# Four row tiles for two outer products, and three other numbers for the planner that orders the kernel

## The chip, the core and the metric

The kernel runs on one core of one Trainium2 chip. Its time is device microseconds of an execution, and the figure compared is the median of several runs. Of one execution there is also a profile: every instruction of every engine with its start and end. The engines are PE (matrix products), PEld (PE's loading of the stationary operand), DVE and ACT (element by element work), POOL (a slower helper) and SP (issues most transfers).

## The reference

Two branches read the same 2048 tokens of width 640 and are mixed by a gate for each token, `g = sigmoid(sum(x * gate_w))`.

```python
x = A_u
g = _sigmoid((x * gate_w).sum(-1, keepdims=True))
a = _A_ref(x, ...)                     # long convolution
b = relu(x @ w1) @ w2                 # network, 640 -> 1728 -> 640
return g * a + (1 - g) * b

# _A_ref: for each of 640 channels d a filter K[d, l] over l = 0 .. 2047
A = -exp(log_A_real) + 1j * A_imag
C = (C_real + 1j * C_imag) * exp(log_dt)[:, None]
P = exp((A * dt[:, None])[:, :, None] * l)
K = 2 * einsum("dn,dnl->dl", C, P).real        # n = 0 .. 127
y = causal convolution of x with K (by FFT), + x * D_skip
```

Each tap of a filter is a sum over 128 complex exponentials. With l written as 32 a + b (64 values of a, 32 of b) an exponential is a coarse factor in a times a fine factor in b, so a filter is a product of two small matrices of cosines, sines and decays.

## The kernel before

The work falls into three kinds, which share one core and are interleaved by a planner written in the kernel.

**The network** (`feed_forward`; tile names pf, h, hw, w1, w2, q). All its products are split into a high and a low part in a reduced float32 format, three products for one. The 1728 inner features are done in three parts of 5, 5 and 4 blocks of 128. `wide` multiplies x by w1 for 512 tokens (products of 512 columns), ACT takes relu and the high part, DVE the low part; `sums` multiplies by w2 (products of 320 columns) and adds to the running result q, which waits in memory between parts.

**Generating the taps** (`ssm`). The 640 channels go in 40 chunks c of 16. The logarithms and phases of a chunk, split into 8 rows a channel (128 rows), are read back from memory as a tile PS for four chunks at a time (`load_rows`, queue "rows"). `phases` and `exponents` then form, as outer products with a constant table `tg`, for each of the 128 values of n and each channel: pg (64 numbers: 32 fine phases and 32 of 64 coarse ones), px (64: coarse decays) and pe (32: fine decays). The table is block-diagonal: a channel's 8 rows meet its own columns and zeros elsewhere. ACT rounds pg to whole turns (cs, `whole`), DVE subtracts (sn), ACT takes exp of pe and px (me, mg) and sine and cosine, DVE multiplies them into factors (`factors`: G, mg, cs, sn). `taps` multiplies the factors of two chunks (pk), DVE transposes them (kt), POOL adds D_skip, and they go to memory (kd). The products of one chunk, pg, px and pe, stand together ("a visit", 40 of them).

**The convolution** (`conv`). It replaces the FFT by four stages of small products on tiles of the array: `stage1` (operands tf and ck, cl or xu; tiles of 64 rows and 64 columns), `stage2` (tm; 64x32), `inv2` (tn; 32x64) and `inv1` (tw; 128x64), in five blocks of 128 channels. All write tiles called pc. One call of `inv2` issues 64 products, which the profile records as 128, since it shows two for each product in plain float32.

**The order.** The class `Plan` holds tasks with an engine, a queue, an estimated duration, what they wait for, what buffers they take, and a rank. `run` simulates all engines and writes the instructions in the order found; each engine then executes its own in program order, whatever the real times are. PE has a mode for each kind of tiling: "f" for full products, "c" and "c1" for the convolution, "t" for taps; `CHANGE` is what a switch costs in the plan. `run` also counts PE's instructions, in blocks of 128, and lets PE wait in the plan where a block would be used up before the next is fetched (`FETCH`, `BUSY`, lines 274 to 282 before). Transfers land after their size over a `RATE` for their queue. `CG` says for each of eight groups of 256 tokens how many of the five channel blocks are joined on the network's way out (q, POOL in `joined` and `with_last`) and how many on the convolution's (yo, POOL in `inv1`).

PSUM has eight banks: before, pg and px have two each, pe and pk one each, and pf two; the convolution's pc follows where the generation's were.

## Time and profile before

| | |
|---|---|
| median of 3 runs | 622.47 us (621.3 to 626.9) |
| the profiled execution's own time | 632.85 us |
| its span, first to last instruction | 631.1 us |
| granted TensorE clock, mean | 0.992 |
| busy PE, PEld, DVE, ACT, POOL | 609.0, 481.6, 507.9, 399.0, 92.4 us |

The profiled execution is 10.4 us longer than the median. Rows of the profile name an operation by its engine and by the tiles it writes and reads (out<-in). "L322" is one helper line that records every operation, so tiles tell them apart. A bracket behind a row of the timeline is the time for which the engine was idle before, and what ended it; "issue" there means that nothing the profile shows released the engine. A matrix product's end is modelled and products overlap, so the step from one start to the next is what a product costs PE.

### The profile page before, as it was taken

How to read it: one execution, taken by the hardware profiler on the slowest of the kernel's cores; microseconds unless marked ns; L12 is line 12 of the kernel's file. 1: busy time of each engine (PE TensorE's matmuls, PEld its weight loads, DVE VectorE, ACT ScalarE, POOL GpSimd, SP SyncE). 2: the span in 40 equal slices, each digit the busy share in tenths (PEclk: the TensorE clock that was granted, in tenths of full speed). 3: DMA queues.
4: the chain of work that ended last, by engine and by line, in shares of the span. 5: the costliest groups of instructions: out<-in, count | busy, mean ns of one | idle time of the engine just before them, and what ended most of it. 6: DMA issues, size and time to landing. Idle time of an engine off the chain costs nothing.

```text
span 631.1 us, 18316 instructions
## 1 busy us (share of the span) xinstructions
PE 609.0 (97%) x7864; PEld 481.6 (76%) x7864; DVE 507.9 (80%) x794; ACT 399.0 (63%) x579; POOL 92.4 (15%) x133
## 2 busy tenths in 40 slices
PE   7999989999999999999999999999979999989997
PEld 5998969888988988988988988755656465656656
DVE  5998559898999889999999998568676757746842
ACT  6578369997999888788789796023225342342470
POOL 0000000000000000000000000007060180361744
PEclk9999989998999999999999999999999999999999
DMA  9993933913656435535442243781543534563343
GB/s 292 386 371 116 406 102 115 301 58 109 195 184 242 153 108 205 153 112 177 133 144 81 64 162 116 234 339 30 194 127 126 183 103 136 185 221 102 115 149 119
DMA packets 54153, 108.05 MB, mean 171 GB/s; under 512 B 5432, under 2 KB 29880, under 8 KB 53176
## 3 DMA queue, kind: packets, MB, share of 16 engines
q1 hardware_dynamic: 53848, 106.63, 50.4%
q8 instruction: 62, 1.02, 0.7%
q10 hardware_dynamic: 224, 0.25, 0.1%
q14 instruction: 19, 0.16, 0.1%
HBM read 67.79 MB, written 39.06 MB: 169 GB/s over the span
## 4 chain that ended last, share of the span: by engine, by line
PE 78%; DVE 11%; DMA 5%; ACT 3%; issue 2%; POOL 0%; SPq 0%; DVEq 0%; ACTq 0%
PE pf L322 47%; PE pc L322 18%; PE pk L322 6%; PE pg L322 3%; PE px L322 2%; PE pe L322 1%; DMA ws<-in_B_w_dram 1%; DVE hwl L322 1%; DVE mg L322 1%; DVE sn L322 1%; DVE G L322 1%; DMA ps<-hl 1%; DMA xu<-in_x_dram 1%; DMA ws<-in_w_dram 1%; DMA PS<-ps 1%
## 5 line engine op out<-in xcount | busy, mean ns | idle before, releaser
L322 PE MATMUL pf<-xx,w1h 128*128 128x512 f32 x560 | 175.5, 399 | 1.7 <-DVE w1h L322 1.0
L322 PEld LDWEIGHTS pf<-xx,w1h 128*128 128x128 f32 x560 | 102.6, 189 | 37.2 <-issue 12.6
L322 PE MATMUL pf<-xx,w1l 128*128 128x512 f32 x260 | 102.1, 393 | 0.0
L322 ACT COPY ku<-pc 128x512 f32<-128x512 f32 (+1 forms) x60 | 43.8, 758 | 74.0 <-PE pc L322 63.4
L322 POOL TENSOR_TENSOR ku<-ku 128x256 f32<-128x256 f32 x80 | 56.2, 744 | 86.2 <-DVE ku L322 56.8
L322 POOL TENSOR_TENSOR kt<-kt,dsk 128x8 f32<-128x8 f32 x20 | 9.3, 466 | 393.0 <-DVE kt L322 211.6
L322 DVE STREAM_TRANSPOSE ku<-pc 128x512 f32<-128x512 f32 x80 | 50.8, 687 | 15.4 <-PE pc L322 15.2
L322 DVE TENSOR_TENSOR ku<-pc,ku 128x512 f32<-128x512 f32 x80 | 52.8, 686 | 11.0 <-ACT ku L322 9.6
L322 PE MATMUL pf<-w2l,hh 128*128 128x320 f32 x192 | 59.2, 312 | 1.9 <-issue 1.9
L322 PE MATMUL pf<-w2h,hh 128*128 128x320 f32 x192 | 59.7, 315 | 0.8 <-DVE q L322 0.8
L322 PE MATMUL pf<-w2h,hwh 128*128 128x320 f32 x192 | 59.7, 312 | 0.7 <-ACT hwh L322 0.7
L322 PE MATMUL pf<-w2l,hwh 128*128 128x320 f32 x192 | 59.9, 313 | 0.0
L322 PE MATMUL pf<-w2h,hwl 128*128 128x320 f32 x192 | 58.1, 316 | 1.9 <-DVE hwl L322 1.9
L322 ACT CAST cs<-pg 128x1024 int32<-128x1024 f32 x40 | 40.4, 1010 | 29.5 <-PE pg L322 29.4
L322 PEld LDWEIGHTS pf<-xx,w1l 128*128 128x128 f32 x260 | 49.0, 188 | 11.0 <-DVE w1l L322 0.3
L322 DVE TENSOR_TENSOR sn<-pg,cs 128x1024 f32<-128x1024 f32 x40 | 48.6, 1215 | 7.5 <-ACT cs L322 7.4
L322 ACT ACT_TABLE_LOAD x42 | 53.9, 1283 | 0.7
L322 DVE TENSOR_TENSOR mg<-mg,cs 128x1024 f32<-128x1024 f32 x40 | 49.0, 1224 | 2.9 <-ACT cs L322 1.0
L322 PE MATMUL pf<-w2h,hl 128*128 128x320 f32 x160 | 48.1, 317 | 0.0
L322 ACT ACTIVATE cs<-cs,half_pi 128x1024 f32<-128x1024 f32 x40 | 45.7, 1142 | 0.0
L322 PE MATMUL pc<-ku,tm 64*32 64x256 f32 x1280 | 42.9, 392 | 2.7 <-issue 2.4
L322 ACT ACTIVATE mg<-px 128x1024 f32<-128x1024 f32 x40 | 41.3, 1033 | 1.8 <-PE pk L322 1.8
(151 smaller groups left out, 1260.4 us busy)
## 6 DMA issues: line engine op xcount, KB each, us to landing
xx<-xt SPq DMA_DIRECT2D x24, 640.0 KB, 4.7
xt<-xx SPq DMA_DIRECT2D x16, 640.0 KB, 8.8
part<-q SPq DMA_DIRECT2D x16, 640.0 KB, 3.3
q<-part SPq DMA_DIRECT2D x16, 640.0 KB, 4.9
xl<-in_u_r_dram SPq DMA_DIRECT2D x16, 320.0 KB, 3.1
kd<-kt SPq DMA_DIRECT2D x80, 64.0 KB, 2.5
xu<-in_u_b_dram SPq DMA_DIRECT2D x5, 1024.0 KB, 4.9
xu<-in_x_t_dram SPq DMA_DIRECT2D x6, 640.0 KB, 6.8
```

Source lines behind the costliest of these rows:

```text
L322: self._last = self._tc.keep_in_program_order(f(*a, **k))
```

## The change

Four things change together.

1. `phases` issues pg and px as four products, each of 32 rows (4 channels) with 512 columns (64 of pg and 64 of px for each of its 4 channels), into four banks of one tile, where there were two products of 128 rows for pg and two for px. Each of the four uses its own 32 rows of the array. The table holds 4 channels' columns in place of 16, so `tg` falls from 2560 columns to 1024 and `spread`, which builds it on ACT, from 32 instructions to 20. pe stays a full product. ACT's and DVE's readers see the halves of the four banks (`quads`). One tile and one token now stand for pg and px. The visit's first task has a mode "g" of its own.
2. In `run`, where a task of the convolution would be held up by the fetch of instructions for more than `STALL` (0.3), a ready network product is taken in its place; `FETCH` goes from 2.4 to 3.0.
3. Reloads of PS are counted as landing 2.5 us later (`LAND`).
4. `CG` goes from (0,0,0,0,1,2,5,5) to (0,0,0,0,1,3,5,5).

```diff
-CG = (0,0,0,0,1,2,5,5)
+CG = (0, 0, 0, 0, 1, 3, 5, 5)
...
-    FETCH = 2.4
+    FETCH = 3.0
     BUSY = 2.6
     SLACK = .8
-    MARGIN = 0
+    STALL = .3
+    LAND = dict(rows=2.5)
...
+                if e == 'PE' and t.mode in self.BURST and done + t.n >= 128:
+
+                    end = start + t.dur * (128 - done) / t.n
+                    if block + self.FETCH + (self.BUSY if dma > end + 2 else 0) - end > self.STALL:
+                        other = [x for x in c if x[1].mode == 'f' and x[0] <= start + .05]
+                        if other:
+                            r, t = min(other, key=lambda x: key(x[1]))
+                            start = max(at, r)
...
-                t.end = max(dma, start + t.dur) + 1.15 + self.MARGIN
+                t.end = max(dma, start + t.dur) + 1.15 + self.LAND.get(t.q, 0)
...
+        quads = lambda x: x.rearrange("p (m d) j -> p m (d j)", m=4)
...
-                p = self.psg.tile([128, 4, 256], F32, name="pg")
-                pf = p.rearrange("p d j -> p (d j)")
-                st['pg'] = pf.rearrange("p (d j) -> p d j", j=64)
-                for h in range(2):
-                    x = slice(h * 512, h * 512 + 512)
-                    self.E.matmul(pf[:, x], R[c], self.tg[:, x], start=True, stop=True)
+                p = self.psg.tile([128, 4, 512], F32, name="pg")
+                st['pg'], st['px', c] = p[:, :, :256], p[:, :, 256:]
+                for m in range(4):
+                    x = slice(32 * m, 32 * m + 32)
+                    self.E.matmul(p[:, m], R[c][x], self.tg[x, :512], start=True, stop=True)
...
-            a = visit[c, 1] = A('PE', None, 0.46, pe, [rd, opened, *self.tg_done], take=[p_], use=[r_], rank=GPR, mode='f')
+            a = visit[c, 1] = A('PE', None, 0.26, pe, [rd, opened, *self.tg_done], take=[p_, px_], use=[r_], rank=GPR, mode='g', n=4)
...
-                p = self.psg.tile([128, 4, 256], F32, name="px")
-                pf = p.rearrange("p d j -> p (d j)")
-                st['px', c] = pf.rearrange("p (d j) -> p d j", j=64)
-                for h in range(2):
-                    x = slice(h * 512, h * 512 + 512)
-                    self.E.matmul(pf[:, x], R[c], self.tg[:, 1024 + h * 512:1536 + h * 512], start=True, stop=True)
                 q = st['pe', c] = self.psg.tile([128, C, 32], F32, name="pe")
-                self.E.matmul(q.rearrange("p d j -> p (d j)"), R[c], self.tg[:, 2048:], start=True, stop=True)
+                self.E.matmul(q.rearrange("p d j -> p (d j)"), R[c], self.tg[:, 512:], start=True, stop=True)
...
-            a = visit[c, 2] = A('PE', None, 0.69, pe, [rd, opened, *self.tg_done], take=[p_], use=[r_], rank=GPR, mode='f')
+            a = visit[c, 2] = A('PE', None, 0.24, pe, [rd, opened, *self.tg_done], use=[p_, r_], rank=GPR, mode='f', n=1)
```

The planner's order moves on all engines. Three places on PE follow, each before and then after the change. The helper's line is L332 in the changed kernel; pf<-xx are products of `wide`, pf<-w2 products of `sums`, and numbers in names tell buffers apart.

The first place is the first visit of the generation, on PE. Before:

```order
L322 MATMUL pf<-xx,w1h_205 128x512 x2
L322 MATMUL pf<-xx,w1l_206 128x512
L322 MATMUL pg<-tg,PS 128x512 x2
L322 MATMUL px<-tg,PS 128x512 x2
L322 MATMUL pe<-tg,PS 128x512
L322 MATMUL pf<-xx,w1h_205 128x512 x2
L322 MATMUL pf<-xx,w1l_206 128x512
```

After:

```order
L332 MATMUL pf<-xx,w1h_205 128x512 x2
L332 MATMUL pf<-xx,w1l_206 128x512
L332 MATMUL pf<-xx,w1h_205 128x512 x2
L332 MATMUL pf<-xx,w1l_206 128x512
L332 MATMUL pf<-xx,w1h_212 128x512 x2
L332 MATMUL pf<-xx,w1l_213 128x512
L332 MATMUL pg<-tg,PS 128x512 x4
L332 MATMUL pe<-tg,PS 128x512
L332 MATMUL pf<-xx,w1h_212 128x512 x2
L332 MATMUL pf<-xx,w1l_213 128x512
```

The visit has four products of pg in place of two and two, and twelve network products of 512 columns that followed it now stand ahead of it (the rest of the block of w1h_205 and the first three of w1h_212).

The second place is where `inv2` (pc<-ku,tn) of the first channel block meets `stage2` (pc<-ku,tm) of the second, on PE. Before:

```order
L322 MATMUL pc<-ku,tn 64x128 x64
L322 MATMUL pc<-ku,tm 32x256 x48
L322 MATMUL pf<-w2l_4798,w2h_5603 128x320
L322 MATMUL pf<-w2h_4797,w2l_5604 128x320
L322 MATMUL pf<-w2h_4675,hh_5253 128x320
```

After:

```order
L332 MATMUL pc<-ku,tn 64x128 x64
L332 MATMUL pf<-w2l_4783,w2h_5551 128x320
L332 MATMUL pf<-w2h_4782,w2l_5552 128x320
L332 MATMUL pc<-ku,tm 32x256 x48
L332 MATMUL pf<-w2h_4588,hh_5201 128x320
```

Two network products moved from behind the first 48 products of `stage2` to between the two bursts.

The third place is the first half of `inv2` of the fourth channel block, on PE, with the end of `inv1` (pc<-ku,tw) of the block before. Before:

```order
L322 MATMUL pc<-ku,tm 32x256 x32
L322 MATMUL pc<-ku,tw 64x512 x2
L322 MATMUL pf<-w2h_4752,w1l_6728 128x320
L322 MATMUL pf<-w2h_4797,w2h_6753 128x320
L322 MATMUL pf<-w2l_4798,w2h_6753 128x320
L322 MATMUL pf<-w2h_4797,w2l_6754 128x320
L322 MATMUL pc<-ku,tw 64x512 x2
L322 MATMUL pc<-ku,tn 64x128 x64
L322 MATMUL pf<-w2h_4675,hh_6387 128x320
```

After, from the last of the twelve network products that now stand between the halves of the 64:

```order
L332 MATMUL pf<-w2h_4782,w2l_6860 128x320
L332 MATMUL pc<-ku,tn 64x128 x32
L332 MATMUL pf<-w2h_4588,hh_6341 128x320
L332 MATMUL pf<-w2l_4589,hh_6341 128x320
L332 MATMUL pf<-w2h_4588,hl_6342 128x320
L332 MATMUL pf<-w2h_4599,hh_6568 128x320
L332 MATMUL pf<-w2l_4600,hh_6568 128x320
L332 MATMUL pc<-ku,tw 64x512 x8
```

The 64 products of `inv2`, which stood in one burst, are two bursts of 32 with network products between them, and the products of `inv1` follow behind five more.

More of the change, by code (lines that the diff above doesn't have):

```diff
@@ L102, in tables @@
     tg[np.arange(16), :, 160 + np.arange(16)] = 1
+    tg[np.arange(16), :, 176 + np.arange(16) % 4] = 1
     f = lambda x: np.ascontiguousarray(x.astype(np.float32))
-    return dict(t_g=f(tg.reshape(128, 176)), t_f1=f(np.tile(np.stack([f1, f1[slots()]], axis=1), (2, 1, 1))), t_w=f(w.reshape(128, 64)),
+    return dict(t_g=f(tg.reshape(128, 180)), t_f1=f(np.tile(np.stack([f1, f1[slots()]], axis=1), (2, 1, 1))), t_w=f(w.reshape(128, 64)),
                 t_m=f(m.reshape(128, 32, 64)), t_n=f(n.reshape(128, 8, 2, 2, 64)))
@@ L948, in steps_in @@
         def steps_in():
[L949 removed]
+            tl['tgs'] = self.prm.tile([128, 180], F32, name="tgs")
             D_.dma_start(tl['tgs'], io['t_g'])
@@ L962, in params @@
             self.late_loads.append(a)
-        for d in range(0, 16, 2):
-            self.tg_done.append(A('ACT', 'tg', 1.1, spread(range(d, d + 2)), [a], rank=TGA))
+        for d in range(0, 16, 4):
+            self.tg_done.append(A('ACT', 'tg', 1.1 if d else 2.2, spread(range(d, d + 4)), [a], rank=TGA))
         return [*done, *self.tg_done]
```

23 lines of the change are left out of this document (12 added, 11 removed).

## The prediction

> **What bounds the kernel now.** I read the page first, for which engine is full and for how long.
>
> ```profile
> span 631.1 us, 18316 instructions
> PE 609.0 (97%) x7864; PEld 481.6 (76%) x7864; DVE 507.9 (80%) x794; ACT 399.0 (63%) x579; POOL 92.4 (15%) x133
> PE   7999989999999999999999999999979999989997
> DVE  5998559898999889999999998568676757746842
> PE 78%; DVE 11%; DMA 5%; ACT 3%; issue 2%; POOL 0%; SPq 0%; DVEq 0%; ACTq 0%
> ```
>
> PE is busy 97% of the span and carries 78% of the chain that ended last. DVE, with 80% overall, is at 8 or 9 tenths from the sixth slice to the 25th and lower after it. Those are two stages: the taps are generated until about 403 us, then they are convolved. So I split the span there, with the table of busy times by window.
>
> ```profile
> 85.00:160.00 75.00, 73.44 (x844) 63.99 (x843) 67.02 (x95) 67.94 (x86) 1.90 (x4) 0.97 0.40 129
> 160.00:385.00 225.00, 224.26 (x2831) 197.62 (x2829) 215.70 (x323) 196.66 (x224) 6.65 (x14) 1.00 0.45 148
> 385.00:403.40 18.40, 17.88 (x346) 16.66 (x345) 13.55 (x23) 4.02 (x5) 0.57 (x1) 1.00 0.70 212
> 403.40:631.10 227.70, 214.58 (x3439) 134.25 (x3437) 147.41 (x239) 80.66 (x164) 82.41 (x107) 0.99 0.47 155
> 160.00:200.00 40.00, 40.00 (x445) 34.96 (x444) 39.29 (x56) 37.46 (x47) 0.91 (x2) 1.00 0.64 213
> ```
>
> After the window and its length come PE, PEld, DVE, ACT and POOL busy, then the granted clock. In the generation (first three rows, 318.4 us) PE works 73.44 + 224.26 + 17.88 = 315.6 us and DVE 67.02 + 215.70 + 13.55 = 296.3 us. PE is the bound there, but DVE has only 22.1 us of idle time in all. In the convolution (fourth row) DVE has 80 us to spare and PE 13.1 us of visible idle. This is the main fact of the case: work taken from PE in the generation is worth at most what DVE can give back.
>
> **Part 1: phases and coarse decays on four row tiles.** One of the 40 visits, from the timeline of PE:
>
> ```profile
> 212.22 0.62 PE L322 MATMUL pg<-tg,PS 128*128 128x512 f32 x2
> 212.68 0.62 PE L322 MATMUL px<-tg,PS 128*128 128x512 f32 x2
> 213.14 0.40 PE L322 MATMUL pe<-tg,PS 128*128 128x512 f32 x1
> 213.38 0.31 PE L322 MATMUL pf<-w2h,hl 128*128 128x320 f32 x1
> ```
>
> From 212.22 to 213.38 it is 1.16 us: five products of 512 columns at 0.23 us each. Afterwards pg and px come from four products, each on 32 rows of the array, and pe from one full one. No row shows a tile of 32 rows by 128 columns, so the price has to be built. Other tiles show what running side by side and changing the tiling cost:
>
> ```profile
> 409.31 0.39 PE L322 MATMUL pf<-xx,w1l 128*128 128x512 f32 x1
> 409.63 3.71 PE L322 MATMUL pc<-xu,tf 64*64 64x512 f32 x32
> 413.27 0.73 PE L322 MATMUL pf<-xx,w1h 128*128 128x512 f32 x2
> 413.84 0.40 PE L322 MATMUL pf<-xx,w1l 128*128 128x512 f32 x1
> 417.51 0.62 PE L322 MATMUL pf<-xx,w1h 128*128 128x512 f32 x2
> 417.96 0.39 PE L322 MATMUL pf<-xx,w1l 128*128 128x512 f32 x1
> 418.28 1.95 PE L322 MATMUL pc<-ck,tf 64*64 64x512 f32 x16
> 420.16 0.73 PE L322 MATMUL pf<-xx,w1h 128*128 128x512 f32 x2
> ```
>
> Thirty-two records on 64x64 tiles take 3.64 us until the next full product (413.27 less 409.63), sixteen take 1.88 us. Sixteen more, four sets of four tiles, therefore cost 1.76 us: 0.44 us a set. The fixed part inside is 1.88 − 1.76 = 0.12 us. The step into the tiles is 0.32 us instead of 0.23, 0.09 more. After the return two products take 0.57 us (413.27 to 413.84) instead of 0.45 (417.51 to 417.96), 0.12 more. A round trip into tiles and back costs 0.09 + 0.12 + 0.12 = 0.33 us.
>
> The set of four itself: at best one full product's step, 0.23 us; at worst four steps in a row, 0.92 us (the slower rival below). The row nearest in shape says 0.44, but it is in plain float32, while pg, like pf, multiplies in the reduced format of the 0.23 us step. I take 0.23 and keep 0.44 for the range. A visit becomes 0.23 + 0.23 + 0.33 = 0.79 us, which saves 0.37 us, and 40 of them 14.8 us of PE. With 0.44 it would be 0.16 us each, 6.4 us in all. The Trainium skill (TensorE: Matmul & The Clock Gate, Measured speedup vs the span model) gives 3.07 times for four row tiles of 512 columns: 0.92/3.07 = 0.30 us for the set, an estimate from that page, and 2.8 us less in all; no run shows it yet.
>
> ACT and DVE read the same numbers of elements, now from half of each of four banks, and I price that at nothing. The table t_g shrinks twelve ACT copies of it away, in the first 80 us, where ACT is not on the chain; also nothing.
>
> **Part 2: rows counted as landing later.** The first visit waits for its reload:
>
> ```profile
> 80.35 0.39 PE L322 MATMUL pf<-xx,w1l 128*128 128x512 f32 x1
> 82.72 1.11 PE L322 MATMUL pg<-tg,PS 128*128 128x512 f32 x2 [1.98 <-DMA PS<-ps]
> 83.62 1.06 PE L322 MATMUL px<-tg,PS 128*128 128x512 f32 x2
> 84.48 0.63 PE L322 MATMUL pe<-tg,PS 128*128 128x512 f32 x1
> 82.70:86.30 3.60, 3.58 (x9) 2.85 (x10) 1.31 (x2) 2.36 (x3) 0.00 (x0) 0.53 0.05 19
> ```
>
> PE idles 1.98 us and the following nine products run at a granted clock of 0.53, 0.43 us each instead of 0.23: 1.8 us more. The order now puts twelve more products of 512 columns (12 × 0.23 = 2.7 us) ahead of that visit, so both losses should go, 3.8 us of PE. The landing itself does not move, and it is where DVE's share of the generation begins.
>
> **Parts 1 and 2 together.** The 1.98 us lie ahead of the landing. Between it and the last taps PE needs 14.8 + 1.8 + 2.7 = 19.3 us less. DVE's 296.3 us of work stay (the DVE rows of the new order hold the same operations, about 1 us less of them behind the first sn). PE's share would so fit in 318.4 − 19.3 = 299 us, and DVE needs 296.3 with no idle time at all. The two are level, and DVE becomes the bound as often as PE. What it reaches when pressed: 39.29 of 40 us (98.2%) in its best stretch above, 215.70 of 225 (95.9%) over the long one, where PE was the bound. I take 97.2%: 296.3/0.972 = 304.8 us, **13.6 us less** than 318.4; by the two shares 16.7 and 9.4. The 19.3 us of PE are not all paid out: some 6 us turn into waits of PE for sn, G and mg.
>
> **Part 3: network products where instructions are awaited.** PE's waits that nothing releases, in the convolution:
>
> ```profile
> 452.88 0.70 PE L322 MATMUL pc<-ku,tm 64*32 64x256 f32 x16 [1.32 <-issue]
> 471.79 0.99 PE L322 MATMUL pc<-ku,tn 32*64 32x128 f32 x23 [3.22 <-issue]
> 509.32 0.67 PE L322 MATMUL pc<-ku,tm 64*32 64x256 f32 x13 [1.05 <-issue]
> 560.99 0.41 PE L322 MATMUL pf<-w2l,hh 128*128 128x320 f32 x1 [1.94 <-issue]
> 471.90:475.40 3.50, 3.50 (x33) 3.17 (x34) 1.22 (x3) 2.06 (x2) 0.00 (x0) 0.51 0.59 186
> ```
>
> They sum to 7.5 us, and behind the longest the clock is at 0.51 for 3.5 us, another 1.7: 9.2 us at stake. All lie in or just behind bursts of small tiles, as the rule assumes. The order shows two products put before the first wait's place, more around the others, and nothing changed at the longest: inv2 with 14 network products ahead of it and 12 behind, where 15 and 14 stood. I take 4 us for the profiled execution, between 0 and 9.2. Against it stand the new round trips: seven more changes of tiling in the convolution, 7 × 0.33/2 = 1.2 us. The changed CG moves one 128-column piece of two blocks from one POOL join to another; POOL's 82.41 of 227.7 us hide that. If its cover were gone it would be one POOL addition, under 1 us. SP's four more issues stand in queues that wait for data.
>
> **Sum.** The profiled execution has 632.85 us (1.75 around the span): 632.85 − 13.6 − 4 + 1.2 = 616.5. It is 10.4 us over the median of the runs and above the slowest of them, so part of its awaited instructions and clock drops may be its own. For the runs I count only 2.5 us for part 3: 622.47 − 13.6 − 2.5 + 1.2 = 607.6. I forecast **607 us**.
>
> **Rivals.** *A, DVE keeps up:* the stretch of 98.2% speaks for it. Then all 16.7 us come, and with part 3 whole 9.2 − 1.2 on top: 622.5 − 24.7 = 598, or 595 if the tail of the generation closes as well. Against it: the plan reckons DVE's operations shorter than they are (1.14 for sn in the kernel's own text).
>
> ```profile
> L322 DVE TENSOR_TENSOR sn<-pg,cs 128x1024 f32<-128x1024 f32 x40 | 48.6, 1215 | 7.5 <-ACT cs L322 7.4
> L322 ACT CAST cs<-pg 128x1024 int32<-128x1024 f32 x40 | 40.4, 1010 | 29.5 <-PE pg L322 29.4
> ```
>
> *B, the emptying of PSUM decides:* sn takes 1.22 us, cs 1.01, and now pg is free only when sn and mg have both read it. A PE that runs ahead then stops in program order, with network products behind it. At 95.9% for DVE and nothing from part 3: 622.5 − 9.4 + 1.2 = 614; with the set at 0.44 us PE saves only 6.4 + 1.8 + 2.7 = 10.9 us and it is 613 too. The Trainium skill has this as a rule (TensorEngine Tiling (Array Packing), PSUM Bottleneck): tiling speeds up PE and not the emptying of PSUM, which may become the bottleneck. By that rule B is the case, and DVE's 22.1 us of idle time bear it out half.
>
> *C, given back:* network work ahead of the first convolution product is the same in both orders (649 products of 512 columns and 1024 of 320), so the convolution starts earlier by the whole gain, and its loads of kd, q and xx may not; or the rule for instructions does not do what it says, since the longest wait's place is unchanged. Up to the 13.6 us go again: 616 to 623, no change. The DMA share of 0.47 speaks against it.
>
> *D, slower: the four tiles run one after another.* A visit is then 0.92 + 0.23 + 0.33 = 1.48 us, 0.32 more, on a PE that is already the bound: 40 × 0.32 = 12.8 us, and 622.5 + 12.8 − 2.5 = 633. The turning point is a set of 0.60 us (1.16 − 0.23 − 0.33). The 0.44 us for a set of four 64x64 tiles speaks against it; nothing in the profile shows four tiles of 128 columns each.
>
> **Chances.** Forecast (600 to 612) 0.50; A 0.17; B 0.16; C 0.11; D 0.06. A measurement of this kernel tells about 1% (6.2 us) from no change. Faster by more: the first three, less a little of B, 0.82. Within 1%: C and that rest, 0.12. Slower: D, 0.06. The range runs from 595, where A ends, to 618, which takes in B and the lower end of C; outside are the rest of C, D and a better A, about 2 in 10.
>
> **What would show it.** Part 1: pg's four products starting within 0.05 us and a visit near 0.8 us from pg to the next pf; 1.5 us is D. Parts 1 and 2: no wait of PE for PS near 82 us, last kt near 390 us instead of 403, DVE near 97% between, and waits of PE for DVE of several us in all. If DVE is at 95% and PE still never waits, I have the bound wrong. Part 3: waits on issue in the convolution below 4 us in all. The forecast is wrong if the generation shrinks by under 8 us or over 18, or if the convolution's 227.7 us change by more than 6.

## The result, and the profile after

The changed kernel is slower: 646.59 us median of 4 runs (644.88 to 648.06), beside 624.68 us (621.3 to 629.99) for the kernel before on the same chip, a ratio of 1.030 (95% interval 1.026 to 1.035). I had forecast 607 us. Ratios and intervals, here and below, are formed from the single runs in the faster of two states and are not the quotients of the medians beside them (1.035 here).

The profiled execution of the kernel before that the prediction used (632.85 us) was longer than its runs; a second profile of the same kernel, label `again`, took 624.08 us, close to the median, and the stages are compared with that one. The head of the page of the changed kernel:

```profile
span 643.1 us, 18238 instructions
PE 603.3 (94%) x7864; PEld 461.7 (72%) x7864; DVE 508.7 (79%) x794; ACT 397.2 (62%) x567; POOL 92.3 (14%) x133
PE   8999999999979998999999996998999998998897
DVE  5998559898889898999999898677687775955732
```

PE is busy 5.7 us less than the 609.0 of the first profile and the span is 12 us longer: PE waits. The table of busy times by window says in which stage. First the kernel before (the second profile), from the first sn of the generation to the last taps, and from there to the end; then the same two stages of the changed kernel. The columns are those of the prediction's window table.

```profile
84.90:400.00 315.10, 313.16 (x4014) 275.60 (x4014) 296.18 (x439) 268.32 (x314) 9.12 (x19) 1.00 0.46 149
400.00:622.30 222.30, 213.18 (x3438) 133.07 (x3437) 147.26 (x239) 80.67 (x164) 82.50 (x107) 0.99 0.48 158
```

```profile
86.40:414.10 327.70, 305.00 (x4001) 255.32 (x4000) 295.50 (x437) 269.28 (x313) 8.91 (x19) 0.98 0.44 143
414.10:643.10 229.00, 215.85 (x3438) 133.73 (x3436) 147.59 (x239) 81.22 (x164) 82.55 (x107) 0.98 0.47 154
```

Of the 20.8 us between these two executions (644.88 − 624.08), 12.6 come in the generation (327.7 − 315.1), 6.7 in the convolution (229.0 − 222.3) and 1.5 ahead of both (86.4 − 84.9). In the generation PE is busy 8.2 us less, at a granted clock of 0.98 in place of 1.00, and idles 22.7 us in place of 1.9. DVE's work is the same to 0.7 us; its idle time grew from 18.9 to 32.2 us. No engine is full there any more: PE, DVE and ACT wait for each other. The waits of the changed kernel by engine (total, times, longest) name whom for:

```profile
ACT mg L332 <- DVE sn L332: 18.1, 18, 2.0
```

```profile
PE pg L332 <- ACT mg L332: 11.7, 16, 1.9
PE pk L332 <- DVE cs L332: 5.7, 3, 5.0
PE pg L332 <- DVE sn L332: 3.2, 4, 1.6
```

The wait of mg for sn exists in no profile of the kernel before. The single wait of 5.0 us, of pk for cs, ends at 396.0 us, near the end of the generation. mg reads the px half of the banks and sn the pg half; neither uses what the other makes. The timeline of the changed kernel shows one such loop (rows of ACT, DVE and PE, other work between them left out):

```profile
174.36 1.01 ACT L332 CAST cs<-pg 128x1024 int32<-128x1024 f32 x1
...
176.09 1.22 DVE L332 TENSOR_TENSOR sn<-pg,cs 128x1024 f32<-128x1024 f32 x1
...
177.33 1.02 ACT L332 ACTIVATE mg<-pg 128x1024 f32<-128x1024 f32 x1 [1.46 <-DVE sn L332]
...
178.41 0.50 PE L332 MATMUL pg<-tg,PS 32*128 32x512 f32 x4 [1.44 <-ACT mg L332]
...
178.84 0.50 PE L332 MATMUL pe<-tg,PS 128*128 128x512 f32 x1
...
179.17 0.63 PE L332 MATMUL pf<-xx,w1h 128*128 128x512 f32 x2
```

ACT stands 1.46 us until sn has ended (176.09 + 1.22 = 177.31), and PE 1.44 us until mg has ended (177.33 + 1.02 = 178.35). Emptying the banks of a visit is now cs, sn and mg in series, 1.01 + 1.22 + 1.02 = 3.25 us, where mg could run beside sn before. A longer wait can have a second price: behind the next one (1.87 us, until 189.14) the granted clock is low for 3.5 us. It need not have one: in `again` PE waits 1.9 us for PS, until 83.0 us, and the granted clock from 82.0 to 89.0 us is 1.00.

```profile
192.20:195.70 3.50, 3.50 (x83) 2.85 (x76) 3.46 (x5) 3.49 (x4) 0.16 (x1) 0.56 0.38 153
```

The Trainium skill has the rule (PSUM — Partial Sum Buffer, PSUM bank collisions raise a hardware error): two engines may not touch the same bank in the same partitions at once, two readers included, and the compiler's scheduler adds a dependency between instructions of ACT and DVE on one bank. The trace agrees as far as it can: the 18 waits above. It shows the ordering, not what would happen without it, which wasn't tried.

In the convolution the waits for instructions did not go. PE's waits of the changed kernel and, behind them, of the kernel before in its second profile:

```profile
PE pc L332 <- issue: 6.5, 4, 2.0
PE pc L332 <- ACT yo L332: 1.9, 1, 1.9
```

```profile
PE pc L322 <- issue: 2.1, 1, 2.1
PE pf L322 <- issue: 1.9, 1, 1.9
```

### The profile page after: what moved, and what is told of

Same layout as the page of the kernel before. It is cut to its first block, busy times and chain, and to the rows that moved or that the text cites. A ratio compares the mean times of both kernels' runs of the same rounds, so it can differ in the third digit from the quotient of the medians.

```text
span 643.1 us, 18238 instructions
## 1 busy us (share of the span) xinstructions
PE 603.3 (94%) x7864; PEld 461.7 (72%) x7864; DVE 508.7 (79%) x794; ACT 397.2 (62%) x567; POOL 92.3 (14%) x133
## 3 DMA queue, kind: packets, MB, share of 16 engines
q8 instruction: 62, 1.02, 0.6%
## 5 line engine op out<-in xcount | busy, mean ns | idle before, releaser
L332 PE MATMUL pf<-xx,w1h 128*128 128x512 f32 x560 | 177.9, 405 | 1.0 <-DVE w1h L332 0.9
L332 PEld LDWEIGHTS pf<-xx,w1h 128*128 128x128 f32 x560 | 103.7, 192 | 39.8 <-issue 17.4
L332 PE MATMUL pf<-xx,w1l 128*128 128x512 f32 x260 | 102.3, 394 | 0.0
L332 ACT COPY ku<-pc 128x512 f32<-128x512 f32 (+1 forms) x60 | 44.1, 758 | 69.9 <-PE pc L332 59.2
L332 DVE STREAM_TRANSPOSE ku<-pc 128x512 f32<-128x512 f32 x80 | 50.6, 687 | 23.3 <-PE pc L332 23.3
L332 POOL TENSOR_TENSOR ku<-ku 128x256 f32<-128x256 f32 x80 | 56.2, 737 | 82.0 <-DVE ku L332 59.8
L332 POOL TENSOR_TENSOR kt<-kt,dsk 128x8 f32<-128x8 f32 x20 | 9.1, 456 | 403.9 <-DVE kt L332 274.7
L332 PE MATMUL pf<-w2h,hh 128*128 128x320 f32 x192 | 60.3, 318 | 0.8 <-DVE q L332 0.8
L332 PE MATMUL pf<-w2h,hwl 128*128 128x320 f32 x192 | 57.4, 312 | 3.0 <-DVE hwl L332 3.0
L332 PE MATMUL pf<-w2h,hwh 128*128 128x320 f32 x192 | 59.8, 313 | 0.0
L332 PE MATMUL pf<-w2l,hwh 128*128 128x320 f32 x192 | 59.7, 312 | 0.0
L332 PE MATMUL pf<-w2l,hh 128*128 128x320 f32 x192 | 58.8, 310 | 0.0
L332 DVE TENSOR_TENSOR ku<-pc,ku 128x512 f32<-128x512 f32 x80 | 52.8, 685 | 6.5 <-ACT ku L332 5.3
L332 PEld LDWEIGHTS pf<-xx,w1l 128*128 128x128 f32 x260 | 49.3, 190 | 11.1
L332 DVE TENSOR_TENSOR sn<-pg,cs 128x1024 f32<-128x1024 f32 x40 | 48.8, 1219 | 8.5 <-ACT cs L332 4.8
L332 ACT ACTIVATE mg<-pg 128x1024 f32<-128x1024 f32 x40 | 41.1, 1028 | 19.8 <-DVE sn L332 18.1
L332 DVE TENSOR_TENSOR mg<-mg,cs 128x1024 f32<-128x1024 f32 x40 | 48.9, 1223 | 1.6
L332 ACT CAST cs<-pg 128x1024 int32<-128x1024 f32 x40 | 40.3, 1008 | 15.6 <-PE pg L332 15.4
L332 PE MATMUL pf<-w2h,hl 128*128 128x320 f32 x160 | 47.5, 313 | 0.0
L332 PE MATMUL pk<-mg,cs 128*32 128x64 f32 x1280 | 41.5, 228 | 5.7 <-DVE cs L332 5.7
L332 ACT ACTIVATE cs<-cs,half_pi 128x1024 f32<-128x1024 f32 x40 | 45.6, 1141 | 0.0
```

The lines of the kernel that those rows point to most:

```text
L332: self._last = self._tc.keep_in_program_order(f(*a, **k))
```

## The experiments

Ratios are to the kernel before on the same chip, with 95% intervals, and not all runs were on one chip; a profile is one execution. How far executions of one order differ is seen in seven profiles that have the very same order of PE in the convolution. From the last taps to the end four of them took 218.7 us (`small`, below), 222.3 (`again`), 227.2 (`two64_same`, below) and 227.7 (the first profile); the other three lie between. I therefore put nothing on a difference of under 9 us in that stage of one profile.

**The kernel before, profiled again** (`again`, no edit).

> The kernel before, unchanged, profiled once more, to have a profile nearer to its median than the one of 632.85 us. Every theory expects 621 to 628 us, and the parts that are shorter than in the first profile are what that one had of its own: a wait of 3.2 us for instructions and 5 us of halved clock in the convolution or the generation.

It took 624.08 us. PE's waits for instructions in the convolution are 4.0 us here and were 7.5 us in the first profile, at the same order: a part of what the prediction put "at stake" in part 3 belonged to that execution.

### Which part of the change costs

`tiles_only` is the changed kernel with the planner's old numbers; `plan_only` the kernel before with all of the planner's parts and no tiles.

```diff
--- the changed kernel
+++ tiles_only
-CG = (0, 0, 0, 0, 1, 3, 5, 5)
+CG = (0,0,0,0,1,2,5,5)
-    FETCH = 3.0
-    STALL = .3
-    LAND = dict(rows=2.5)
+    FETCH = 2.4
+    STALL = 1e9
+    LAND = dict()
```

> The changed kernel with the planner's old numbers and without its new rule (FETCH 2.4, no STALL, rows not counted later, old CG): the four row tiles alone. Theory 1 (shared banks): 640 to 655 us, as slow as the whole change, ACT waiting some 18 us for sn before mg. Theory 2 (planner's numbers): 603 to 612 us. Theory 3 (tiles): as theory 1, but with visits that last longer than the 1.16 us of before.

> The kernel before with the planner's part of the change alone: FETCH 3.0, the rule with STALL, rows landing 2.5 us later, and the new CG; pg and px as before. Theory 1 (shared banks): 612 to 623 us, a little faster or the same, waits on issue in the convolution shorter. Theory 2 (the planner's new numbers): 640 us or more, first taps at 110 us or later and a longer convolution. Theory 3 (tiles): as theory 1.

The tiles alone: 639.79 us, 1.022 (1.018 to 1.027). The planner's parts alone: 633.2 us, 1.011 (1.007 to 1.015). Both cost, and the two together (1.033) are about the whole (1.030). Neither half of the change is a gain by itself. For `plan_only` the theory of the shared banks had 612 to 623 us, so that theory alone is not enough.

### What it is about the tiles

`share` has the tiles' layout and no tiles: pg and px in halves of the same four banks, but from four full products of 128 rows, so PE's work is that of the kernel before, and the planner's numbers are the old ones (its order in the generation is another, since pg and px are now one task).

```diff
--- the kernel before
+++ share
...
-                p = self.psg.tile([128, 4, 256], F32, name="pg")
...
-                for h in range(2):
-                    x = slice(h * 512, h * 512 + 512)
-                    self.E.matmul(pf[:, x], R[c], self.tg[:, x], start=True, stop=True)
+                p = self.psg.tile([128, 4, 512], F32, name="pg")
+                st['pg'], st['px', c] = p[:, :, :256], p[:, :, 256:]
+                for m in range(4):
+                    self.E.matmul(p[:, m], R[c], self.tg[:, 512 * m:512 * m + 512], start=True, stop=True)
...
```

> The kernel before with one thing of the change: pg and px of a visit in the two halves of the same four banks, written by four full products of 512 columns (the table is laid out for it, PE does the same work as before). Theory 1 (shared banks: mg on ACT and sn on DVE read the same banks and are made to wait for each other, the plan does not know it): 633 to 648 us, slower by 2 to 4%; ACT's waits for DVE sn before mg rise from nothing to 10 us or more in all. Theory 2 (the planner's new numbers are the cause): 622 us, the same. Theory 3 (the tiles themselves): 622 us, the same.

It is the slowest of all: 647.41 us, 1.034 (1.029 to 1.039). In its profile each reader waits for the other:

```profile
ACT mg L322 <- DVE sn L322: 10.2, 14, 1.4
```

```profile
DVE sn L322 <- ACT mg L322: 13.0, 11, 2.7
```

`two64` is the reverse: the whole change, but with two tiles of 64 rows, so that pg keeps two banks of its own and px two of its own.

```diff
--- the changed kernel
+++ two64
...
-                p = self.psg.tile([128, 4, 512], F32, name="pg")
-                st['pg'], st['px', c] = p[:, :, :256], p[:, :, 256:]
-                for m in range(4):
-                    x = slice(32 * m, 32 * m + 32)
-                    self.E.matmul(p[:, m], R[c][x], self.tg[x, :512], start=True, stop=True)
+                p, q = (self.psg.tile([128, 2, 512], F32, name=k) for k in ("pg", "px"))
+                st['pg'], st['px', c] = p, q
+                for k, y in enumerate((p, q)):
+                    for m in range(2):
+                        x = slice(64 * m, 64 * m + 64)
+                        self.E.matmul(y[:, m], R[c][x], self.tg[x, 512 * k:512 * k + 512], start=True, stop=True)
...
```

> The whole change, but on two row tiles of 64 rows: pg in two banks, then px in two others, each from two products side by side, so that no bank holds both. Changes of tiling as in the change; the set costs one step more, so a visit some 1.0 to 1.1 us. Theory 1 (shared banks): 608 to 620 us, no wait of ACT for sn before mg. Theory 2 (planner's numbers): 640 us or more. Theory 3 (tiles, their drains): 635 us or more.

630.25 us, 1.009 (1.005 to 1.013): not the 608 to 620 us that I expected, but two thirds of the loss are gone, though PE has more work in a visit than in the changed kernel. The planner's parts and PE's order in the convolution are the same in both; the generation took 316.0 us (86.9 to 402.9), and 327.7 in the changed kernel.

That points to the shared banks, but `share` changes several things at once: the readers' order, the readers' layout (half of each bank), that four banks come free together, and with these the planner's order. `small` and `held` separate them, in the kernel before, where pg and px have their own tiles and banks. `small` adds one DVE instruction of one element a row (z) beside each sn; `held` has the same instruction and lets mg add its result, a zero, so that mg and sn of a visit cannot run side by side. In the 8 visits in which mg stands first in the program, z is formed from mg instead, and sn stands behind z. Nothing else differs between the two, the order on PE and DVE included.

```diff
--- the kernel before
+++ small
...
+                    V.tensor_sub(st['sc', c][0], st['pg'], I(st['sc', c][1]))
+                    V.tensor_scalar(z, st['sc', c][0][:, 0, :1], 0.0, None, op0=ALU.mult)
...
--- small
+++ held
-                    V.tensor_scalar(z, st['sc', c][1][:, 0, :1], 0.0, None, op0=ALU.mult)
+                    V.tensor_scalar(z, st['mg', c][:, 0, :1], 0.0, None, op0=ALU.mult)
...
-                        S.activation(st['mg', c], st.pop(('px', c)), AF.Exp)
+                        S.activation(st['mg', c], st.pop(('px', c)), AF.Exp, **(dict(bias=st['z', c]) if ('z', c) in st else {}))
```

> The kernel before with one DVE instruction of one element a row beside each sn, whose result nobody reads. It is the measure for the next run. 40 instructions of 0.05 to 0.1 us: 2 to 4 us of DVE at most; 624 to 629 us, ratio 1.000 to 1.007.

> As the run with the small instruction, but mg adds its result (a zero), so that ACT's mg waits for DVE's sn of its visit (or, where mg stands earlier, sn for mg); pg and px keep their own tiles and banks, and PE's products are the old ones. Theory (the order of the two readers is what shared banks cost): share, where only the banks were shared, took 3.4% more; here 2.5 to 4% over the run with the small instruction, 640 to 652 us, with waits of mg for sn of 15 to 30 us in all. Rival (half banks, or four banks that come free at once, are what cost): within 1% of the run with the small instruction.

`small` took 623.43 us, 0.998 (0.993 to 1.002); `held` 641.29 us, 1.026 (1.018 to 1.034), which is 17.9 us or 2.9% over `small`. The generation in their profiles, `small` and then `held`, from the first sn to the last taps:

```profile
84.70:403.00 318.30, 315.12 (x4015) 276.91 (x4014) 299.10 (x479) 268.58 (x314) 9.14 (x19) 1.00 0.45 147
```

```profile
84.60:417.90 333.30, 320.69 (x4015) 274.77 (x4014) 300.81 (x479) 272.80 (x315) 9.14 (x19) 1.00 0.43 141
```

```profile
ACT mg L322 <- DVE z L322: 18.6, 18, 2.5
```

```profile
DVE z L322 <- ACT mg L322: 4.9, 8, 1.0
```

The wait of one reader for the other, without any shared bank, costs 15.0 us in the generation of these two profiles (that of `held`, 645.90 us, is its longest run), with the same 18 waits of mg and nearly the same sum (18.6 us) as the changed kernel's. That shows that the wait alone can cost what the tiles lost. Layout and joint release need not add anything. (A little of it, 32 times 0.08 us on ACT, is mg's own longer time with the added operand: medians of 1.116 us and 1.034 in `held`.)

It does not show that all of the 2.2% of `tiles_only` is this wait. In its generation PE idles 15.0 us (329.00 − 314.02) where it idles 1.9 in `again`. But it also stands still twice near the end, where `again` has a single wait of 0.8 us: 3.5 us until 616.4 and 5.4 us until 628.3.

```profile
PE pf L332 <- DVE q L332: 5.4, 1, 5.4
PE pc L332 <- DVE ku L332: 4.1, 4, 3.5
```

These 8.9 us need no shared bank, for `light` (below) has the same two waits without one; they come with the order that the planner wrote there. The changed kernel does not have them.

Two ways round the wait. `told` is the changed kernel with the plan told of the wait; `split2_old` has the four row tiles and the old planner, but the banks are two tiles of two, and cs, sn and mg are done in halves, so that mg's first half waits only for sn's first half.

```diff
--- the changed kernel
+++ told
...
-            d = acts[c, 2] = A('ACT', None, 0.96, exps(1), [b], use=[p_, m_], rank=2, mode='exp')
+            d = acts[c, 2] = A('ACT', None, 0.96, exps(1), [b, tasks[c]['sub']], use=[p_, m_], rank=2, mode='exp')
--- tiles_only
+++ split2_old
-                p = self.psg.tile([128, 4, 512], F32, name="pg")
...
+                p = [self.psg.tile([128, 2, 512], F32, name=k) for k in ("pg", "px")]
...
-            d = A('DVE', 'g1', 1.14, lambda: V.tensor_sub(quads(st['sc', c][0]), st['pg'], quads(I(st['sc', c][1]))), [b],
...
+                for h in range(2):
+                    V.tensor_sub(sn[:, 2 * h:2 * h + 2], st['pg'][h], cs[:, 2 * h:2 * h + 2])
...
```

> The changed kernel, with mg given sn among what it waits for in the plan, so that the planner knows of the wait and orders around it. Theory 'the wait is costly because the plan does not know it': 628 to 636 us, PE's waits for mg and sn before pg from 15 us to under 5. Theory 'the wait lengthens the loop pg, cs, sn, mg, pg itself': 642 to 650 us, the waits only moved to other places.

> Four row tiles as in the change and pg and px of a tile still in one bank, but the four banks are two tiles of two banks each, and cs, sn and mg are done in halves, so that mg's first half waits for sn's first half only; planner numbers as before. The halves cost about 0.12 us of DVE and 0.35 us of ACT a visit (40 visits: 5 us of DVE, 14 us of ACT). Theory (the order of readers in a bank costs, by waiting): the same tiles with whole instructions and the old planner measured 1.022; the wait of mg for sn shrinks from about 10 us to a few, but DVE, with 20 us of idle time in the generation, has 5 us more to do, so 1.005 to 1.020, 627 to 637 us. Rival (it is the four-row tiles themselves or the stride of the readers, not their wait): 1.022 or more. Rival (the wait was all of it, and DVE's added work hides): 0.985 to 1.000.

`told`: 638.51 us, 1.024 (1.020 to 1.028), with mg's wait for sn at 22.5 us, between the two ranges that I expected. A plan that knows the wait cannot take it away. PE idles 10.9 us in its generation (88.7 to 423.2) in place of the changed kernel's 22.7, but the two waits near the end stand here too, 7.1 and 5.3 us. `split2_old`: 633.36 us, 1.010 (1.002 to 1.018) beside 1.022 for the same tiles in whole instructions; mg's wait is 6.8 us there and 10.3 in `tiles_only`, and DVE has 5.5 us more to do (301.7 us in the generation, 296.2 before). Stride and tiles are the same in both, so they can explain at most the 1.0% that is left. Of that, the two waits near the end (3.5 and 6.0 us) are larger than DVE's added work; no run parts the rest.

### Was PE the bound?

`light` leaves out two of the five products of every visit: one product of pg and one of px are computed, and ACT and DVE read them twice, so half of the coarse phases and decays are copies and the taps are not the reference's. ACT's and DVE's work stays, PE loses 80 products of 0.23 us, 18.4 us.

```diff
--- the kernel before
+++ light
-                for h in range(2):
-                    x = slice(h * 512, h * 512 + 512)
-                    self.E.matmul(pf[:, x], R[c], self.tg[:, x], start=True, stop=True)
+                st['pg'] = st['pg'][:, None, :8].to_broadcast([128, 2, 8, 64])
+                self.E.matmul(pf[:, :512], R[c], self.tg[:, :512], start=True, stop=True)
...
```

> The kernel before with two of the five products of a visit left out (the second half of pg and of px; the readers read the first half twice, so the taps of half the channels are not the reference's). PE saves 2 x 0.23 us in each of 40 visits, 18.4 us, with no change of tiling, no shared bank and the planner's old numbers; the plan knows the shorter products. Theory 'PE bounds the generation': 604 to 608 us. Theory 'DVE and ACT bound it as soon as PE is lighter', as two64 against plan_only suggests: 614 to 622 us, with PE's waits in the generation grown by 10 us or more.

620.75 us, 0.994 (0.991 to 0.997): 18.4 us of PE were worth 0.6%, some 3.8 us. The two windows of its profile:

```profile
85.30:406.70 321.40, 313.41 (x3998) 277.23 (x3997) 298.25 (x443) 273.84 (x321) 8.99 (x19) 0.98 0.45 151
406.70:619.00 212.30, 201.10 (x3378) 124.26 (x3376) 143.90 (x234) 76.49 (x157) 82.45 (x107) 0.98 0.47 157
```

The planner moved some 13 us of network products (48 of 512 columns, 14 of 320) into the generation, so the stages can't be compared singly. Over both, PE's busy time fell by 11.8 us (514.51, and 526.34 in `again`) and not by 18.4, at granted clocks of 0.98 where they were 1.00 and 0.99; and PE idles 8.0 + 11.2 = 19.2 us in place of 1.9 + 9.1 = 11.0. 11.8 less 8.2 is what remains. So 97% of busy time on PE did not mean that a microsecond of PE is a microsecond of time.

Where PE idles matters for what this shows. In the generation it is 6.1 us more than in `again`. Two waits near the end, until 601.9 and 612.7 us, are another 9.0 us:

```profile
PE pf L322 <- DVE q L322: 5.5, 1, 5.5
PE pc L322 <- DVE ku L322: 3.5, 1, 3.5
```

There the new order has PE's next product wait for DVE. So `light` changes the order along with the work, and how much a microsecond of PE is worth under the old order is not shown: `light` with the plan's durations left as before was not run.

`two64_old` has the 64-row tiles in separate banks with the old planner numbers, and `two64_land` adds only the rows' landing to it. `two64_same` has the same tiles, but every duration and mode of the plan is left as before, so PE's order is the old one.

```diff
--- two64
+++ two64_old
-CG = (0, 0, 0, 0, 1, 3, 5, 5)
+CG = (0,0,0,0,1,2,5,5)
-    FETCH = 3.0
-    STALL = .3
-    LAND = dict(rows=2.5)
+    FETCH = 2.4
+    STALL = 1e9
+    LAND = dict()
--- the kernel before
+++ two64_same
-                    x = slice(h * 512, h * 512 + 512)
-                    self.E.matmul(pf[:, x], R[c], self.tg[:, x], start=True, stop=True)
+                    x, y = slice(h * 512, h * 512 + 512), slice(64 * h, 64 * h + 64)
+                    self.E.matmul(pf[:, x], R[c][y], self.tg[y, :512], start=True, stop=True)
...
```

> The tiles without the shared banks and without any of the planner's parts: two tiles of 64 rows, pg in two banks of its own and px in two of its own, tilings planned with the old numbers, no rule for instructions, rows landing as before, CG as before. Theory (the readers' shared banks and the planner's parts are what costs; the tiles themselves help a little): two64 measured 1.009 and the planner's parts alone 1.011 to 1.014, so without them the ratio should be 0.993 to 1.000, some 620 to 625 us, with no wait of ACT's mg for DVE's sn and PE's waits in the convolution near 5 us. Rival (the planner's parts cost only because they shift the order by chance, and this order is another throw): anything between 0.99 and 1.02, with the difference in the convolution and not in the generation. Rival (even two 64-row tiles cost PE as much as they save): 1.000 to 1.005, the generation's length not under 315 us.

> As the run with two 64-row tiles and the old planner, but rows counted as landing 2.5 us later. If the first visit's wait for its reload (1.98 us, and 1.8 us of slow clock behind it) were worth what the prediction gave it, this is 3 to 4 us faster than the same kernel without that count, about 617 to 621. If the landing of the rows, not PE, sets where the first visit starts, PE only does other work meanwhile and the gain is under 1 us. If it moves the whole order for the worse, it is 2 to 8 us slower, as the other planner parts were.

> Two 64-row tiles for pg and for px in banks of their own, with every duration and mode of the plan left as in the kernel before, so that the order on PE and DVE is the old one (ACT loses some copies of the table). Theory (the tiles help a little, the new order cost): in the two other runs with these tiles pg, px and pe took 6.9 us less of PE and the first network products behind them 3.7 us more, so up to 3 us less: 0.995 to 1.000, 621 to 625 us. Rival (the tiles themselves cost, by the change of tiling in the generation): 1.005 to 1.012, as with the tiles and the old planner.

`two64_old`: 634.06 us, 1.011 (1.004 to 1.018), against my expectation of 0.993 to 1.000. `two64_land`: 631.73 us, 1.007 (1.003 to 1.010). `two64_same`: 620.43 us, 0.993 (0.988 to 0.997). PE's products are the same in the three; what differs is the order that the planner writes for other durations, and between the first and the last (each beside the kernel before on its own chip) it is worth 1.8%, more than the tiles gave. The generations of `two64_old` and `two64_same` are alike, 315.0 and 314.3 us by their windows. In the convolution PE goes between network and convolution products 87 times in `two64_old` and 79 times in `two64_same`, as before (counted in the traces); that the loss comes from there is likely, but one profile of each doesn't show it. Here my theory, that only the shared banks and the planner's parts cost, had missed a third item: the order that follows from the new durations.

A visit with these tiles, in the timeline of PE of `two64_same`:

```profile
212.53 0.31 PE L323 MATMUL pf<-w2h,hwh 128*128 128x320 f32 x1
212.77 0.51 PE L323 MATMUL pg<-tg,PS 64*128 64x512 f32 x2
213.12 0.40 PE L323 MATMUL px<-tg,PS 64*128 64x512 f32 x2
213.44 0.50 PE L323 MATMUL pe<-tg,PS 128*128 128x512 f32 x1
213.78 0.31 PE L323 MATMUL pf<-w2l,hwh 128*128 128x320 f32 x1
```

1.01 us from pg to the next pf and 0.09 more on the step in (0.24 in place of 0.15): 1.10 instead of 1.16, 2.4 us over 40 visits. The measured 0.7% (0.3 to 1.2) is not less than that: under the old order this small saving came through.

### The planner's parts

`rule_only` has the rule and FETCH of 3.0, `fetch_only` the figure alone, `land_only` only the rows' landing, all on the kernel before. CG was not run by itself.

```diff
--- the kernel before
+++ rule_only
-    FETCH = 2.4
+    FETCH = 3.0
+    STALL = .3
...
+                if e == 'PE' and t.mode in self.BURST and done + t.n >= 128:
...
--- the kernel before
+++ land_only
+    LAND = dict(rows=2.5)
...
-                t.end = max(dma, start + t.dur) + 1.15 + self.MARGIN
+                t.end = max(dma, start + t.dur) + 1.15 + self.LAND.get(t.q, 0)
```

> The kernel before with FETCH 3.0 and the rule with STALL alone; rows not counted later, old CG, pg and px as before. Theory 'the rule costs more changes of tiling than it saves waits': 629 to 635 us, all of plan_only's 1.1%. Theory 'rows or CG are what costs in plan_only': 618 to 627 us.

> The kernel before with the planner's figure for a fetch of instructions raised from 2.4 to 3.0 us and no rule. Rule and figure together measured 1.014. If the rule costs: 0.998 to 1.005 here. If the figure costs, because every order behind a burst becomes another: 1.008 to 1.016.

> The kernel before with rows counted as landing 2.5 us later, and nothing else. By the prediction 3.8 us of PE (the wait of 1.98 us for the first rows and 1.8 us of slow clock behind it): 620 to 621, ratio 0.994. If it is worth nothing because DVE's work starts with the landing either way: 623 to 626, ratio 0.998 to 1.002. All planner parts together measured 1.011 and the rule for instructions alone 1.014, so if the costs add up, this part and CG should come to -0.3% together, ratio 0.997.

`rule_only`: 632.9 us, 1.014 (1.010 to 1.018). `fetch_only`: 622.97 us, 0.996 (0.992 to 1.000). `land_only`: 623.15 us, 0.993 (0.989 to 0.997). So it is the rule that costs: about 1.8% between `rule_only` and `fetch_only`. PE's waits with the rule:

```profile
PE pc L331 <- issue: 4.7, 3, 2.9
PE pc L331 <- ACT yo L331: 3.4, 1, 3.4
```

The waits for instructions are not shorter than the 4.0 us of `again`, and they stand at other places; one of the convolution's products now waits 3.4 us for its buffer. In the timeline of PE of `rule_only` the longest is inside a burst of `inv2` that the rule left whole: 94 records, the wait, and the other 34 of the 128 that stand for 64 products.

```profile
517.89 1.63 PE L331 MATMUL pc<-ku,tn 32*64 32x128 f32 x94
522.48 0.81 PE L331 MATMUL pc<-ku,tn 32*64 32x128 f32 x34 [2.95 <-issue]
523.22 1.62 PE L331 MATMUL pc<-ku,tm 64*32 64x256 f32 x32
```

The order has 91 passages between network and convolution products in place of 79, and 102 changes of tiling in place of 92 (counted in the traces). That the rule's extra changes and its moved waits make up the whole 1.8% is argued from one profile each and not shown.

The landing of the rows gave 0.7%, near the 3.8 us of the prediction, but how is open: the profile of `land_only` is of its longest run (631.41 us), and in it PE's wait of 1.9 us for PS is gone, but the first sn starts at 86.6 us where it starts at 84.9 in `again`, and a wait of pk for cs has come, until 384.5 us.

```profile
PE pk L323 <- DVE cs L323: 2.6, 1, 2.6
```

### The parts that pay, together

`best` is `two64_same` with the rows' landing; `best_fetch` has FETCH of 3.0 as well.

```diff
--- two64_same
+++ best
+    LAND = dict(rows=2.5)
...
--- best
+++ best_fetch
-    FETCH = 2.4
+    FETCH = 3.0
```

> The two 64-row tiles of pg and px in separate banks with the plan's durations left as before, and rows counted as landing 2.5 us later. If the two gains (0.75% and 0.68%) are separate, as PE's work in the visits and PE's wait at the first visit are: 0.984 to 0.990, 614 to 621 us. If both fill the same slack, because DVE or the landing then sets the generation's end: 0.991 to 0.995.

> The same with the planner's figure for a fetch of instructions at 3.0 us. Alone it measured 0.996 (0.992 to 1.000). If that is a gain of its own: 0.981 to 0.988. If it is one more throw of the order behind bursts: anywhere from 0.980 to 1.000, with the generation as long as in the other run.

`best`: 622.36 us, 0.994 (0.990 to 0.997). `best_fetch`: 624.2 us, 0.996 (0.992 to 1.000). The gains don't add up: each of `two64_same`, `land_only` and `best` is 0.7% faster than the kernel before, within 1% and so little more than these measurements can tell. The generation of `best`:

```profile
86.10:399.40 313.30, 307.60 (x3998) 256.11 (x3997) 293.80 (x437) 266.87 (x313) 9.39 (x19) 0.99 0.46 150
```

PE has 5.6 us less to do than in `again`, and the stage is 1.8 us shorter; PE idles 5.7 us in place of 1.9. No version found here is faster by more than 1%.

## Why the prediction was wrong

**The step that failed** is the sentence "ACT and DVE read the same numbers of elements, now from half of each of four banks, and I price that at nothing". The number of elements is right, and the durations too (sn 1.22, mg 1.02, cs 1.01 us). What I didn't ask is who else reads those banks. With one reader in pg's banks and another in px's, sn and mg run side by side; with both in the same banks they stand in line. `share` prices the layout, with its order, at 1.034 and `held` the wait alone at 2.9%, 17.9 us. Instead of nothing the term is some +15 us in the generation (`held` beside `small`), the size of my whole gain there and of the other sign. In the changed kernel itself the generation grew by 12.6 us over `again`, where I had it shrink by 13.6.

**The tiles themselves** were nearly as priced. The first visit in the timeline of PE of the changed kernel, whose wait for PS is gone:

```profile
84.40 0.39 PE L332 MATMUL pf<-xx,w1l 128*128 128x512 f32 x1
84.72 0.51 PE L332 MATMUL pg<-tg,PS 32*128 32x512 f32 x4
```

The step in is 0.32 us, the 0.09 more that I took; pg to pe is 0.43 (178.41 to 178.84 above) and pe to the next pf 0.33. A visit is 0.09 + 0.43 + 0.33 = 0.85 us, not 0.79, and the saving 12.4 us, not 14.8. What was too small is the set of four: 0.43 less the fixed 0.12 is 0.31 us, where I took 0.23 and the estimate from the Trainium skill's page (TensorE: Matmul & The Clock Gate, Measured speedup vs the span model) was 0.30. "A visit near 0.8 us from pg to the next pf" is 0.76. Rival D, the tiles one after another, is refuted, and with it the only way to a slower kernel that I had worked out, at 6 in 100.

**Rival B came near and stopped short.** It says that "now pg is free only when sn and mg have both read it", and stops at when the banks come free. It priced that by DVE's worst share, 95.9%. The worse half, that sn and mg also wait for each other, stood a step further. DVE's share became 295.50 of 327.70, 90.2%, below both ends I had taken from stretches in which no such wait existed. The mark "DVE is at 95% and PE still never waits" did not occur: PE waits 22.7 us, and for mg above all.

**"Work taken from PE in the generation is worth at most what DVE can give back"**, I wrote, and set 13.6 us for 19.3 us of PE. `light` shows 3.8 us for 18.4, without any shared bank. DVE's limit is not what kept the rest: in the generation of `light` DVE has 23.2 us of idle time (298.25 of 321.40), more than the 18.9 of `again`. What kept it is, as far as the profiles show, waits between engines in an order that the planner wrote anew, 9.0 us of them at the end of the kernel; the prediction had no term for a new order. That the chain through all three engines and not PE was the bound under the old order is argued and not shown.

**Part 3**, "network products where instructions are awaited", is the second term with the wrong sign: it was booked as −4 us (−2.5 for the runs) and measured +1.4% alone (`rule_only`), about 8.7 us. Rival C had the words, "the rule for instructions does not do what it says", but no price above zero. I had seen that the longest wait's place was unchanged and that the order has seven more changes of tiling; they should have weighed more than the intention. `again` also shows that 3.5 of the 7.5 us at stake were that execution's own. PE's waits for instructions in the convolution of the changed kernel sum to 6.5 us; the sign that I had named was less than 4.

**Part 2** came out in the size forecast, 3.8 us and 0.7% or some 4.3 us measured, but that may be luck. The wait for PS did go; the 1.8 us of slow clock behind it, which I had counted, are not in `again`, and the first sn came later, not earlier.

## What to carry to other kernels

Before outputs are packed into a bank, ask who reads it: two engines that emptied two tiles side by side will stand in line when the tiles share banks, and no elements need be added for that. That an engine is busy 97% of the time does not say what a microsecond of its work is worth; take work from it in an experiment first, and leave the order as it was while doing so, which `light` did not. And where a planner writes the order, try a cheaper instruction under the old order before changing the planner's figures: the new order is an edit of its own, here worth more than the instruction.

## What was not expected of the hardware

The waits of PE for instructions are not tied to the order alone: with the same order in the convolution they came to 4.0 us in one execution (`again`) and 7.5 in another (the first profile), in the second profile at two places of the order (450 and 551 us), in the first at the same two (453 and 561 us) and at two more (472 and 509 us). The order itself was dearer than expected: the same instructions on PE in another order cost 1.8% (`two64_old` and `two64_same`).
